# TensorE operands placed at chosen addresses modulo 256 bytes in a gated attention and MLP kernel

## The chip, the cores and the metric

The kernel runs on one core of one Trainium2 chip. The metric is the device time of one execution in microseconds (us). Three runs of the kernel before took 436.31, 436.49 and 436.5 us; their median is 436.49 us. A profile of one further execution is the basis of everything that is read from a trace below.

A core has five engines that work side by side and meet at semaphores: TensorE (PE in the profile; its weight loads have a row of their own, PEld), VectorE (DVE), ScalarE (ACT), GpSimd (POOL) and SyncE (SP), whose queue issues all of this kernel's DMA transfers. SBUF is the on-chip memory of 128 partitions; a tile has an address in bytes within each partition, and it is this address that the change is about. PSUM is the memory that TensorE accumulates into.

A matmul has two operands in SBUF. The **loaded** operand (128 columns here) is put into the array by a weight load before the matmul; the **streamed** operand (448, 450 or 512 columns here) is then passed through it. In the call `nc.tensor.matmul(out, a, w)` the first operand `a` is loaded and the second, `w`, is streamed.

## The reference

Shapes: 2048 tokens of width D = 448, 16 heads of 28, a hidden width F of 1792, everything in fp32.

```python
g = sigmoid((x * gate_w).sum(-1, keepdims=True))
# attention: 8 keys per token at distances 0, 2, 4, ... 14, masked before the start
q, k, v = split(x @ wqkv)                      # 16 heads of 28
logits = einsum("bhsd,bhswd->bhsw", q, k[idx]) * 28 ** -0.5
a = einsum("bhsw,bhswd->bhsd", softmax(mask(logits)), v[idx]) @ wo
# MLP
h = relu(x @ w1 + b1) ** 2
b = h @ w2 + b2
out = g * a + (1 - g) * b
```

## The kernel before

**Arithmetic.** Each fp32 operand is split in two halves of a narrower type (`fp32r`), a rounded one (`...h`) and the remainder (`...l`), and a product is three matmuls: h·h, h·l and l·h. The width of 448 is three blocks of 128 rows and one of 64. The last block is handled with both halves stacked (`x7`, `x8`, `w17`, `wo7`), or, in the qkv projection, by running two matmuls at once on the upper and lower 64 rows of the array.

**Stages.** The 2048 tokens are four chunks of 512.

1. *qkv.* The chunks 0, 1, 2, 3 are projected in this order. Chunk 0 starts with 36 matmuls on the full array (`qkv_first`, line 244); all else, 936 matmuls, is issued by `side_by_side` (line 176) in 468 pairs, one of a pair on array rows 0 to 63 and the other on rows 64 to 127. Loaded are 128 tokens of the chunk (`x.h`, `x.l`, `x7`, `x8`), streamed are `wqh`, `wql`, `w7h`, `w7l`: 450 columns for q (two of them are the gate), 448 for k and v. In chunk 0 both matmuls of a pair mostly stream the same block of the weights for different tokens; in chunks 1 to 3 (`qkv_two`) they stream different blocks. ScalarE copies the results to staging tiles, and SP stores them to DRAM. SP also spills the split x of chunks 0 to 2 to DRAM (`x_d`).
2. *Attention* runs on POOL, DVE and ACT beside the matmuls of the later stages, in pieces that a generator emits by a clock of TensorE's planned time (`advance`). Its outputs are tiles `o`, nine of them.
3. *MLP.* The chunks go in the order 3, 0, 1, 2 (`ORDER`). Chunk 3 is still in SBUF; the others are reloaded from `x_d` by `x_reload` into a ring of five slots (`RING`), four in `xpool` and the fifth in the pool of this stage. For each of 14 blocks f of the hidden width, `mlp_h` (line 620) runs 11 matmuls of 512 columns: loaded is a block of `w1h`, `w1l` or `w17`, streamed is x. ACT and DVE turn the result into `hh` and `hl` (lines 626 to 629), and two blocks later `mlp_o` (line 684) runs 12 matmuls of 448 columns: loaded are `hh` or `hl`, streamed is block f of w2, which lies in `w2ah`, `w2al` for f below 7 and in `w2bh`, `w2bl` from 7 on. One such round of 11 and 12 matmuls is called a step below; there are 56.
4. *Output projection.* Once half of attention is done, each step of MLP also takes one tile of 128 tokens: four transposes (lines 702, 703; streamed is `ident`), and 11 matmuls of 448 columns (line 725; loaded are `oh`, `ol`, `o7`, `o8`, streamed are `woh`, `wol`, `wo7`). Eight tiles go beside chunk 1 of MLP, the other eight after chunk 2, and the last 24 matmuls of MLP come at the end.

The order of the instructions on each engine is written out by the code (`tc.manual_schedule()`); semaphores follow from which tile is read and written. Tiles are placed one after another in the order of the code, pool by pool:

```python
    w1h = const.tile([P, 3, F], F32R, name="w1h")
    b1t = const.tile([P, NF], F32, name="b1t")
    wqh = ap.tile([P, 3, 3, NQ], F32R, name="wqh")
    xt = (xpool if r < 4 else bp).tile([P, 2, CH], F32R, tag=f"x{r}", name=f"x{c}b_{j}")
    w2bh = bp.tile([P, NFA, D], F32R, name="w2bh")
```

The pool `ap` (qkv's weights, x of chunks 0 and 2, the staging tiles) is closed after qkv, and the pool `bp` of MLP takes its place in SBUF; a tile of `bp` waits for the last users of what lay there.

Of the kernel before, what the change touches and what calls it, by code (L numbers as in the profile page):

```python
# [15 lines left out]
P = 128  # L16
# [6 lines left out]
NF = F // P  # L23
CH = 512
NQ = D + 2
SCALE = float(DH) ** -0.5


# [23 lines left out]
def gated_mix_kernel(ctx: ExitStack, tc: tile.TileContext, xT, wqkv, w1, w2, wo, b1, b2, out):  # L52
    nc = tc.nc

    def f32(ap):
        return ap.bitcast(F32)
# [101 lines left out]

    def ncols(b):
        return NQ if b == 0 else D  # L160

    class Acc:

# [25 lines left out]
    def qkv_evacuate(pt, c, tl, b):  # L189
        par, t = c // 2, (c % 2) * 4 + tl  # L190
        first = (b, t // 2) not in stage
        if first:
            stage[b, t // 2] = ap.tile([P, G, 2, C], F32, tag="stage", name=f"st{c}_{tl}_{b}", bufs=ST_BUFS)
        st = stage[b, t // 2]
        nc.scalar.activation(st[:, :, t % 2], pt[:, :D].rearrange("p (g c) -> p g c", g=G), AF.Copy)  # L195
        if not first:
            stage.pop((b, t // 2))
            t0 = t - t % 2
            dst, off = ((q_d, 0), (k_d, HALO), (v_d, HALO))[b]
            dd = dst[par, :, off:off + SP].rearrange("g (p s) c -> p g s c", s=NS)[:, :, t0:t0 + 2]  # L200
            nc.sync.dma_start(dd.rearrange("p g s c -> p g (s c)"), st.rearrange("p g s c -> p g (s c)"))
        if b == 0:
            nc.scalar.activation(zt[:, par, t:t + 1], pt[:, D:D + 1], AF.Copy)

    def full(x, acc, tl, b, ks=range(3)):
        sl, n = slice(tl * P, tl * P + P), ncols(b)
        r = []
        for k in ks:
            r += [(acc, x.h[k][:, sl], wqh[:, k, b, :n]), (acc, x.h[k][:, sl], wql[:, k, b, :n]),
                  (acc, x.l[k][:, sl], wqh[:, k, b, :n])]  # L210
        return r

    def last(x, acc, tl, b):

        sl, n = slice(tl * P, tl * P + P), ncols(b)
# [63 lines left out]
    def halo_ap(d, par, g):  # L279
        base = d[par, g].rearrange("r c -> (r c)")  # L280
        return bass.AP(tensor=base.tensor, offset=base.offset, ap=[[NS * C, P], [1, (NS + HALO) * C]])

    def att_load_qk(par, g):
        q = attp.tile([P, NS, C], F32, tag="q", name=f"q{par}{g}")
        k = attp.tile([P, NS + HALO, C], F32, tag="k", name=f"k{par}{g}")
        nc.sync.dma_start(q, q_d[par, g].rearrange("(p s) c -> p s c", s=NS))
        nc.sync.dma_start(k, halo_ap(k_d, par, g))
        return q, k

    def att_load_v(par, g):  # L290
        v = attp.tile([P, NS + HALO, C], F32, tag="v", name=f"v{par}{g}")
        nc.sync.dma_start(v, halo_ap(v_d, par, g))
        return v

# [54 lines left out]

    def gates(par):  # L350

        e = smp.tile([P, NS], F32, tag="e", name=f"e{par}")
# [152 lines left out]
        raws.append(raw)  # L505
    raw7 = attp.tile([P, D], F32, tag="q", name="wqraw7")
    nc.sync.dma_start(raw7, wqkv[2, :, 3, :D])
    x = x_tiles(0, ap)
    for k in range(3):
        nc.scalar.activation(wqh[:, k, 0], raws[0][:, k, :NQ], AF.Copy)  # L510
        parts = (slice(0, 256), slice(256, CH)) if k == 0 else (slice(0, CH),)
        nc.vector.tensor_copy(x.h[k][:, parts[0]], rx[:, k, parts[0]])
        nc.vector.tensor_sub(wql[:, k, 0], raws[0][:, k, :NQ], f32(wqh[:, k, 0]))  # L513
# [4 lines left out]
    split_full(raws[0][:, 3, :NQ], w7h[:, 0], w7l[:, 0])  # L518
    split_x78(rx[:, 3], x.x7, x.x8)

    def wq_split(b, k):
        if k < 3:
            split_full(raws[b][:, k], wqh[:, k, b, :D], wql[:, k, b, :D])
        else:
            split_full(raw7, w7h[:, 1, :D], w7l[:, 1, :D])

# [77 lines left out]
    def x_reload(i, j):  # L604

        c = ORDER[i]
        r = (4 * i + j) % RING
        xt = (xpool if r < 4 else bp).tile([P, 2, CH], F32R, tag=f"x{r}", name=f"x{c}b_{j}")
        nc.sync.dma_start(f32(xt), x_d[c, j])
        return xt  # L610

    hs = {}

    def mlp_h(x, c, f):
        pt = ps("m", f"h{c}_{f}")
# [5 lines left out]
        return pt  # L621

    def mlp_act(pt, c, f):
        hh = bp.tile([P, CH], F32R, tag="hh", name=f"hh{c}_{f}", bufs=3)
        hl = bp.tile([P, CH], F32R, tag="hl", name=f"hl{c}_{f}", bufs=3)
        nc.scalar.activation(pt, pt, AF.Relu, bias=b1t[:, f:f + 1])  # L626
        nc.scalar.activation(hh, pt, AF.Square)  # L627
        nc.scalar.activation(pt, pt, AF.Square)  # L628
# [140 lines left out]

    pend = []  # L770
    early = RING - 4
    nxt = []
# [74 lines left out]
```

## Time and profile before

| | |
|---|---|
| median of three runs | 436.49 us |
| the profiled execution, its own time | 436.64 us |
| its span, from the first instruction to the last | 434.9 us |
| PE busy | 429.1 us (99% of the span), 2516 matmuls |
| PEld busy | 385.9 us (89%) |
| POOL, DVE, ACT busy | 274.8, 257.9, 179.3 us |
| granted TensorE clock, mean over the span | 0.998 |

The page of the profile gives busy times of the engines, the span in 40 slices, the DMA queues, the chain of work that ended last, the costliest groups of instructions by line, and the DMA issues. Matmuls overlap in the record (each is shown from its first column to its last result), so the mean duration of one is longer than the distance to the next. What a matmul costs where PE never waits is that distance. The view that shows it is the chain of waits in order of time: while the chain runs on PE, a piece such as "PE b L684 x12" gives when the piece began and how long these 12 matmuls held the chain.

### The profile page before, as it was taken

The numbers are of one execution on the slowest core, as the hardware profiler recorded it, in microseconds if no ns is written. First come the engines' busy times: TensorE is split into PE (matmuls) and PEld (weight loads), VectorE is DVE, ScalarE is ACT, GpSimd is POOL, SyncE is SP. The second block draws the span as 40 slices with busy tenths as digits, with TensorE's granted clock in tenths as the row PEclk, the third lists the DMA queues.
The fourth block names the chain that finished last, engine by engine and source line by source line (L and its number), as shares of the span: only waits on it lengthen the run. The fifth ranks groups of instructions, "written<-read, shape, count | busy, mean of one in ns | idle before, by whom it ended". The sixth has DMA issues, their size and how long they took to land.

```text
span 434.9 us, 6554 instructions
## 1 busy us (share of the span) xinstructions
PE 429.1 (99%) x2516; PEld 385.9 (89%) x2516; DVE 257.9 (59%) x384; ACT 179.3 (41%) x372; POOL 274.8 (63%) x167
## 2 busy tenths in 40 slices
PE   8999999999999999999999999999999999999996
PEld 7999999999888888888888888888888888888895
DVE  4421322375589977976646776644676856755453
ACT  3542454444554444533433454333523433334530
POOL 1000001940999999999998897945499998785000
PEclk9999999999999999999999999999999999999999
DMA  7989899938723307703203651401427400210013
GB/s 224 365 299 346 223 391 287 356 80 298 260 89 119 142 2 259 254 29 121 78 2 121 223 199 36 151 21 44 142 86 260 172 1 0 76 68 0 2 63 128
DMA packets 33199, 65.44 MB, mean 150 GB/s; under 512 B 2704, under 2 KB 26256, under 8 KB 32784
## 3 DMA queue, kind: packets, MB, share of 16 engines
q1 hardware_dynamic: 33168, 65.02, 43.0%
q8 instruction: 20, 0.33, 0.3%
q14 instruction: 11, 0.09, 0.1%
HBM read 41.23 MB, written 23.77 MB: 149 GB/s over the span
## 4 chain that ended last, share of the span: by engine, by line
PE 97%; DMA 1%; DVE 1%; SPq 0%; issue 0%; ACT 0%
PE h L620 33%; PE b L684 31%; PE qkv L176 22%; PE a L725 8%; PE oT L702 1%; PE qkv L244 1%; DMA xraw<-xT 1%; PE oT L703 0%; SPq L499 0%; SPq L494 0%; DVE bt L660 0%; DVE wql L513 0%; DVE x L514 0%; DVE ol L102 0%; ACT o L101 0%
## 5 line engine op out<-in xcount | busy, mean ns | idle before, releaser
L308 POOL TENSOR_TENSOR qk<-q,k 128x896 f32<-128x896 f32 x64 | 138.6, 2193 | 103.4 <-DMA k<-k_d 72.5
L315 POOL TENSOR_TENSOR av<-lg,v 128x896 f32<-128x896 f32 x64 | 122.3, 2006 | 13.2 <-DVE o L321 7.1
L626 ACT ACTIVATE h<-h,b1t 128x512 f32<-128x512 f32 x56 | 37.0, 662 | 157.6 <-PE h L620 157.6
L176 PE MATMUL qkv<-wqh,x 64*128 64x448 f32 (+1 forms) x528 | 86.8, 363 | 0.0
L629 DVE TENSOR_TENSOR hl<-h,hh 128x512 fp32r<-128x512 f32 x56 | 38.6, 688 | 62.1 <-ACT h L628 61.9
L309 DVE TENSOR_REDUCE lg<-qk 128x32 f32<-128x896 f32 x64 | 66.9, 1076 | 3.9 <-POOL qk L308 3.9
L321 DVE TENSOR_REDUCE o<-av 128x112 f32<-128x896 f32 x64 | 66.6, 1072 | 0.0
L176 PEld LDWEIGHTS qkv<-wqh,x 64*128 64x128 f32 x528 | 59.6, 185 | 0.6
L176 PE MATMUL qkv<-wql,x 64*128 64x448 f32 (+1 forms) x264 | 56.5, 363 | 0.0
L195 ACT ACTIVATE st<-qkv 128x448 f32<-128x448 f32 x48 | 24.7, 544 | 48.4 <-PE qkv L176 39.9
L684 PE MATMUL b<-w2bl,hh 128*128 128x448 f32 x112 | 40.9, 365 | 0.0
L684 PE MATMUL b<-w2bh,hl 128*128 128x448 f32 x112 | 40.9, 365 | 0.0
L684 PE MATMUL b<-w2bh,hh 128*128 128x448 f32 x112 | 40.9, 365 | 0.0
L684 PE MATMUL b<-w2ah,hh 128*128 128x448 f32 x112 | 40.7, 364 | 0.0
L684 PE MATMUL b<-w2ah,hl 128*128 128x448 f32 x112 | 40.6, 362 | 0.0
L684 PE MATMUL b<-w2al,hh 128*128 128x448 f32 x112 | 40.5, 362 | 0.0
L627 ACT ACTIVATE hh<-h 128x512 fp32r<-128x512 f32 x56 | 33.6, 599 | 3.6 <-DMA v_d<-st 1.9
L628 ACT ACTIVATE h<-h 128x512 f32<-128x512 f32 x56 | 33.2, 593 | 0.0
L176 PEld LDWEIGHTS qkv<-wql,x 64*128 64x128 f32 x264 | 30.8, 185 | 0.3
L620 PE MATMUL h<-x1b,w1h 128*128 128x512 f32 x84 | 28.6, 395 | 0.0
L620 PE MATMUL h<-x2b,w1h 128*128 128x512 f32 x84 | 28.5, 393 | 0.0
L620 PE MATMUL h<-x0b,w1h 128*128 128x512 f32 x84 | 28.4, 391 | 0.0
(108 smaller groups left out, 761.0 us busy)
## 6 DMA issues: line engine op xcount, KB each, us to landing
k<-k_d SPq DMA_DIRECT2D x8, 840.0 KB, 5.1
v<-v_d SPq DMA_DIRECT2D x8, 840.0 KB, 4.6
x_d<-x SPq DMA_DIRECT2D x12, 512.0 KB, 5.5
q_d<-st SPq DMA_DIRECT2D x8, 448.0 KB, 8.0
k_d<-st SPq DMA_DIRECT2D x8, 448.0 KB, 5.1
v_d<-st SPq DMA_DIRECT2D x8, 448.0 KB, 6.7
w1raw<-w SPq DMA_DIRECT2D x4, 896.0 KB, 9.9
q<-q_d SPq DMA_DIRECT2D x8, 448.0 KB, 3.4
```

The source lines that it names most:

```text
L176: nc.tensor.matmul(acc.pt[:, :acc.n], a[rows], w[rows], start=acc.todo == 21, stop=acc.todo == 1)
L308: nc.gpsimd.tensor_mul(pr, q[:, s:s + 1].to_broadcast([P, W, C]), k[:, s:s + W])
L309: pending.append(lambda: nc.vector.tensor_reduce(lg[:, s], pr.rearrange("p w (h d) -> p w h d", h=HG), axis=AX.X, op=ALU.add))
L315: nc.gpsimd.tensor_mul(pr.rearrange("p (h d) w -> p w h d", h=HG), lg[:, s][:, :, :, None].to_broadcast([P, W, HG, DH]), v[:, s:s + W].rea ...
L321: pending.append(lambda: nc.vector.tensor_reduce(o[:, g * C:(g + 1) * C], pr, axis=AX.X, op=ALU.add))
L620: nc.tensor.matmul(pt, w, a, start=i == 0, stop=i == len(pr) - 1)
L626: nc.scalar.activation(pt, pt, AF.Relu, bias=b1t[:, f:f + 1])
L627: nc.scalar.activation(hh, pt, AF.Square)
L628: nc.scalar.activation(pt, pt, AF.Square)
L629: at(HL_DELAY, lambda: nc.vector.tensor_sub(hl, pt, f32(hh)))
L684: nc.tensor.matmul(bps[tl][:, :D], a[:, sl], w, start=f == 0 and i == 0, stop=f == NF - 1 and i == 2)
L725: nc.tensor.matmul(pa[:, :D], a, w, start=i == 0, stop=i == len(pr) - 1)
```

## The change

All of it is about where tiles lie. The instructions of TensorE, VectorE, ScalarE and GpSimd are the same ones in the same order with the same shapes. On SP's queue one transfer changes its place: the first reload of x (the first of chunk 0) is issued before the load of w2's row 4 instead of after it, and takes over its wait for the end of qkv on TensorE.

- `wqh` and `wql` get one row of 512 + 2·448 columns for each k block instead of three blocks of 450, and `w7h`, `w7l` one of 512 + 448; the new `block(b)` gives the columns of a block. Every block then starts at the same address modulo 256 bytes.
- `b1t`, the gates (`zt`, `gt`, `g1t`, now parts of one tile `zg`), the tiles of k and v, and `e` are padded to multiples of 256 bytes, and three empty tiles (`pad_x`, `pad_a`, `pad_b`) shift what lies behind them.
- Pools are split, so that x and the staging tiles of qkv (`xap`), MLP's weights with the fifth slot of the ring (`bw`), and `hh`, `hl` (`hp`) can be shifted apart.
- The nine tiles `o` move from a pool of their own, kept through the whole kernel, to MLP's pool `bp`.

Where the operands then start, modulo 256 bytes, as the two programs place them:

| operand | its part | before | after |
|---|---|---|---|
| `wqh`, `wql` (line 176, 244) | streamed | 64, 72, 80 ... 128 and 160, 168 ... 224, by block | 128 |
| `w7h`, `w7l` (line 176) | streamed | 0, 8, 32, 40 | 128 |
| x of chunks 0 and 2 in qkv | loaded | 64 | 64 |
| x of chunks 1 and 3 in qkv | loaded | 128 | 128 |
| `w1h`, `w1l`, `w17` (line 620) | loaded | 128 | 128 |
| x of chunk 3, four slots of the ring (line 620) | streamed | 128 | 128 |
| fifth slot of the ring: block 0 of chunk 0, block 1 of chunk 1, block 2 of chunk 2 (3 of the 11 matmuls of a step each) | streamed | 64 | 128 |
| `hh`, `hl` (line 684) | loaded | 64 | 64 |
| `w2ah`, `w2al` (f below 7) | streamed | 128 | 128 |
| `w2bh`, `w2bl` (f from 7 on) | streamed | 64 | 128 |
| `oh`, `ol`, `o7`, `o8` (line 725); `o`, `od` (lines 702, 703) | loaded | 64 | 64 |
| `woh`, `wol`, `wo7` (line 725) | streamed | 64 | 128 |
| `ident` (lines 702, 703) | streamed | 192 | 128 |

```diff
+NP = 512
...
-    b1t = const.tile([P, NF], F32, name="b1t")
+    b1t = const.tile([P, 64], F32, name="b1t")[:, :NF]
...
-    zt = const.tile([P, 2, NS], F32, name="zt")
-    gt = const.tile([P, 2, NS], F32, name="gt")
-    g1t = const.tile([P, 2, NS], F32, name="g1t")
-
+    zg = const.tile([P, 8, NS], F32, name="zg")
+    zt, gt, g1t = zg[:, 0:2], zg[:, 2:4], zg[:, 4:6]
+
+    const.tile([P, 64], F32, name="pad_x")
...
-    opool = ctx.enter_context(tc.tile_pool(name="opool", bufs=1))
...
+    xap = actx.enter_context(tc.tile_pool(name="phase_a_x", bufs=1, reuse_waits="tile"))
...
-    wqh = ap.tile([P, 3, 3, NQ], F32R, name="wqh")
-    wql = ap.tile([P, 3, 3, NQ], F32R, name="wql")
-
-    w7h = ap.tile([P, 2, NQ], F32R, name="w7h")
-    w7l = ap.tile([P, 2, NQ], F32R, name="w7l")
+    wqh = ap.tile([P, 3, NP + 2 * D], F32R, name="wqh")
+    wql = ap.tile([P, 3, NP + 2 * D], F32R, name="wql")
+
+    w7h = ap.tile([P, NP + D], F32R, name="w7h")
+    w7l = ap.tile([P, NP + D], F32R, name="w7l")
+    ap.tile([P, 48], F32, name="pad_a")
...
+    def block(b):
+
+        o = (0, NP, NP + D)[b]
+        return slice(o, o + ncols(b))
...
-            stage[b, t // 2] = ap.tile([P, G, 2, C], F32, tag="stage", name=f"st{c}_{tl}_{b}", bufs=ST_BUFS)
+            stage[b, t // 2] = xap.tile([P, G, 2, C], F32, tag="stage", name=f"st{c}_{tl}_{b}", bufs=ST_BUFS)
...
-            r += [(acc, x.h[k][:, sl], wqh[:, k, b, :n]), (acc, x.h[k][:, sl], wql[:, k, b, :n]),
-                  (acc, x.l[k][:, sl], wqh[:, k, b, :n])]
+            r += [(acc, x.h[k][:, sl], wqh[:, k, n]), (acc, x.h[k][:, sl], wql[:, k, n]),
+                  (acc, x.l[k][:, sl], wqh[:, k, n])]
...
-        h, l = w7h[:, b // 2, :n], w7l[:, b // 2, :n]
+        sl = slice(tl * P, tl * P + P)
+        n = block(1) if b == 2 else slice(0, ncols(b))
+        h, l = w7h[:, n], w7l[:, n]
...
+    def kv_tile(tag, name):
+        n = (NS + HALO) * C
+        return attp.tile([P, n + 48], F32, tag=tag, name=name)[:, :n].rearrange("p (s c) -> p s c", c=C)
...
-    x = x_tiles(0, ap)
+    x = x_tiles(0, xap)
...
-        xs[c] = x_tiles(c, xpool if c % 2 else ap)
+        xs[c] = x_tiles(c, xpool if c % 2 else xap)
...
+    bw = ctx.enter_context(tc.tile_pool(name="weights_b", bufs=1, reuse_waits="tile"))
+    hp = ctx.enter_context(tc.tile_pool(name="hidden", bufs=3, reuse_waits="tile"))
     bp = ctx.enter_context(tc.tile_pool(name="phase_b", bufs=1, reuse_waits="tile"))
-    w2bh = bp.tile([P, NFA, D], F32R, name="w2bh")
-    w2bl = bp.tile([P, NFA, D], F32R, name="w2bl")
-    woh = bp.tile([P, 3, D], F32R, name="woh")
-    wol = bp.tile([P, 3, D], F32R, name="wol")
-    wo7 = bp.tile([P, D], F32R, name="wo7")
+    opool = bp
+    w2bh = bw.tile([P, NFA, D], F32R, name="w2bh")
+    w2bl = bw.tile([P, NFA, D], F32R, name="w2bl")
+    woh = bw.tile([P, 3, D], F32R, name="woh")
+    wol = bw.tile([P, 3, D], F32R, name="wol")
+    wo7 = bw.tile([P, D], F32R, name="wo7")
...
-        xt = (xpool if r < 4 else bp).tile([P, 2, CH], F32R, tag=f"x{r}", name=f"x{c}b_{j}")
+        xt = (xpool if r < 4 else bw).tile([P, 2, CH], F32R, tag=f"x{r}", name=f"x{c}b_{j}")
...
+    nxt = [x_reload(1, j) for j in range(RING - 4)]
+    bw.tile([P, 48], F32, name="pad_b")
...
-        hh = bp.tile([P, CH], F32R, tag="hh", name=f"hh{c}_{f}", bufs=3)
-        hl = bp.tile([P, CH], F32R, tag="hl", name=f"hl{c}_{f}", bufs=3)
+        hh = hp.tile([P, CH], F32R, tag="hh", name=f"hh{c}_{f}")
+        hl = hp.tile([P, CH], F32R, tag="hl", name=f"hl{c}_{f}")
...
-        if i < 3:
+        if 0 < i < 3:
             nxt = [x_reload(i + 1, j) for j in range(early)]
```

More of the change, by code (lines that the diff above doesn't have):

```diff
@@ L205, in full @@
     def full(x, acc, tl, b, ks=range(3)):
-        sl, n = slice(tl * P, tl * P + P), ncols(b)
+        sl, n = slice(tl * P, tl * P + P), block(b)
         r = []
         for k in ks:
-            r += [(acc, x.h[k][:, sl], wqh[:, k, b, :n]), (acc, x.h[k][:, sl], wql[:, k, b, :n]),
-                  (acc, x.l[k][:, sl], wqh[:, k, b, :n])]
+            r += [(acc, x.h[k][:, sl], wqh[:, k, n]), (acc, x.h[k][:, sl], wql[:, k, n]),
+                  (acc, x.l[k][:, sl], wqh[:, k, n])]
         return r
     def last(x, acc, tl, b):
-        sl, n = slice(tl * P, tl * P + P), ncols(b)
-        h, l = w7h[:, b // 2, :n], w7l[:, b // 2, :n]
+        sl = slice(tl * P, tl * P + P)
+        n = block(1) if b == 2 else slice(0, ncols(b))
+        h, l = w7h[:, n], w7l[:, n]
         return [(acc, x.x7[:, sl], h), (acc, x.x7[:, sl], l), (acc, x.x8[:, sl], h)]
@@ L281, in halo_ap @@
         return bass.AP(tensor=base.tensor, offset=base.offset, ap=[[NS * C, P], [1, (NS + HALO) * C]])
+    def kv_tile(tag, name):
+        n = (NS + HALO) * C
+        return attp.tile([P, n + 48], F32, tag=tag, name=name)[:, :n].rearrange("p (s c) -> p s c", c=C)
     def att_load_qk(par, g):
         q = attp.tile([P, NS, C], F32, tag="q", name=f"q{par}{g}")
-        k = attp.tile([P, NS + HALO, C], F32, tag="k", name=f"k{par}{g}")
+        k = kv_tile("k", f"k{par}{g}")
         nc.sync.dma_start(q, q_d[par, g].rearrange("(p s) c -> p s c", s=NS))
@@ L290, in att_load_v @@
     def att_load_v(par, g):
-        v = attp.tile([P, NS + HALO, C], F32, tag="v", name=f"v{par}{g}")
+        v = kv_tile("v", f"v{par}{g}")
         nc.sync.dma_start(v, halo_ap(v_d, par, g))
@@ L350, in gates @@
     def gates(par):
-        e = smp.tile([P, NS], F32, tag="e", name=f"e{par}")
+        e = smp.tile([P, 32], F32, tag="e", name=f"e{par}")[:, :NS]
         nc.scalar.activation(e, zt[:, par], AF.Exp, scale=-1.0)
@@ L507, in gated_mix_kernel @@
     nc.sync.dma_start(raw7, wqkv[2, :, 3, :D])
-    x = x_tiles(0, ap)
+    x = x_tiles(0, xap)
     for k in range(3):
-        nc.scalar.activation(wqh[:, k, 0], raws[0][:, k, :NQ], AF.Copy)
+        nc.scalar.activation(wqh[:, k, :NQ], raws[0][:, k, :NQ], AF.Copy)
         parts = (slice(0, 256), slice(256, CH)) if k == 0 else (slice(0, CH),)
         nc.vector.tensor_copy(x.h[k][:, parts[0]], rx[:, k, parts[0]])
-        nc.vector.tensor_sub(wql[:, k, 0], raws[0][:, k, :NQ], f32(wqh[:, k, 0]))
+        nc.vector.tensor_sub(wql[:, k, :NQ], raws[0][:, k, :NQ], f32(wqh[:, k, :NQ]))
         nc.vector.tensor_sub(x.l[k][:, parts[0]], rx[:, k, parts[0]], f32(x.h[k][:, parts[0]]))
@@ L517, in gated_mix_kernel @@
             nc.vector.tensor_sub(x.l[k][:, cols], rx[:, k, cols], f32(x.h[k][:, cols]))
-    split_full(raws[0][:, 3, :NQ], w7h[:, 0], w7l[:, 0])
+    split_full(raws[0][:, 3, :NQ], w7h[:, :NQ], w7l[:, :NQ])
     split_x78(rx[:, 3], x.x7, x.x8)
@@ L522, in wq_split @@
         if k < 3:
-            split_full(raws[b][:, k], wqh[:, k, b, :D], wql[:, k, b, :D])
+            split_full(raws[b][:, k], wqh[:, k, block(b)], wql[:, k, block(b)])
         else:
-            split_full(raw7, w7h[:, 1, :D], w7l[:, 1, :D])
+            split_full(raw7, w7h[:, NP:], w7l[:, NP:])
     def when(t, fn, *args):
```

1 line of the change is left out of this document (removed).

## The prediction, made before the changed kernel was run

> **What bounds the kernel now.** I read the page first (busy times, the chain's shares), then the chain of waits in order of time, then the waits of PE.
>
> ```profile
> span 434.9 us, 6554 instructions
> PE 429.1 (99%) x2516; PEld 385.9 (89%) x2516; DVE 257.9 (59%) x384; ACT 179.3 (41%) x372; POOL 274.8 (63%) x167
> PE 97%; DMA 1%; DVE 1%; SPq 0%; issue 0%; ACT 0%
> PE warm L487 <- DVE zero L485: 1.2, 1, 1.2
> ```
>
> PE is busy for 99% of the span, 97% of the chain is PE, and the only wait of PE that the view of waits lists is 1.2 us before the warm-up. So the time is the number of matmuls times their distance, and only that distance can change where the instructions stay the same. It is read from the chain, whose columns are start, us held, what:
>
> ```profile
> 13.81 95.86 PE qkv L176 x928
> 109.67 7.70 PE h L620 x33
> ...
> 124.67 2.49 PE h L620 x11
> 127.16 2.40 PE b L684 x12
> ...
> 149.13 2.49 PE h L620 x11
> 151.62 2.43 PE b L684 x12
> 154.06 2.52 PE h L620 x11
> ...
> 171.44 7.29 PE b L684 x36
> 178.73 7.60 PE h L620 x33
> ...
> 193.67 2.53 PE h L620 x11
> ...
> 248.00 7.64 PE h L620 x33
> ...
> 258.05 2.56 PE h L620 x11
> 260.61 0.33 PE oT L702 x3
> 260.94 0.11 PE oT L703
> ...
> 263.46 2.57 PE h L620 x11
> ...
> 266.47 2.23 PE a L725 x11
> 268.70 2.41 PE b L684 x12
> ...
> 339.06 7.61 PE h L620 x33
> ...
> 349.07 2.54 PE h L620 x11
> ...
> 403.64 0.33 PE oT L702 x3
> ...
> 425.77 4.88 PE b L684 x24
> ```
>
> The reader is to see that the same 11 matmuls cost 2.49, 2.52, 2.53, 2.54, 2.56 or 2.57 us, and the same 12 cost 2.40 or 2.43. Against the table of addresses: 2.40 is w2's first half (streamed at 128), 2.43 its second half (at 64). 2.49 is chunk 3 beside that first half, when every streamed operand of MLP starts at 128; 2.52 is the same chunk with the second half between; 2.53 and more are the chunks with three of 11 matmuls on the fifth slot (at 64). No DMA, wait or clock stands between these rows. So the streamed address bears on the distance, and a matmul streamed at 64 also lengthens those after it: in chunk 3 all 11 are streamed at 128 in both 2.49 and 2.52.
>
> **The change, part by part.** All sums are made against the profiled execution: 436.64 us, of which 434.9 is the span. The median of the runs shown is 0.15 us lower; the difference found here is taken off the median.
>
> *MLP.* After the change every step has the addresses that the five steps from 124.67 to 149.13 have now: 24.46 us, 4.892 per step, of which 2.40 are b and 2.492 are h (226.5 ns per matmul of 512 columns, 200.0 per one of 448). By chunks, from the starts of the chain's pieces:
> - Chunk 3 takes 178.73 - 109.67 = 69.06. I leave the first three h (7.70, with the entry from qkv) as they are; 11 more at 2.492 and 14 b at 2.40 give 68.71: **-0.35**.
> - Chunk 0 takes 248.00 - 178.73 = 69.27; 14 steps of 4.892 are 68.49: **-0.78**.
> - Chunk 1 takes 339.06 - 248.00 = 91.06, with eight tiles of transposes (0.44 each) and of projection (a, 2.23 each). a is 11 matmuls of 448 columns, loaded at 64, streamed at 64 now and at 128 after, as b; 11 at 200.0 ns are 2.20. So 68.49 + 3.52 + 17.60 = 89.61: **-1.45**. The transposes' `ident` moves from 192 to 128, which no row here prices; I take nothing. They would have to move by the whole 8 ns by which the h rows differ per matmul, over 64 of them, to matter by 0.5 us either way.
> - Chunk 2 runs from 339.06 to 403.64, 64.58, with 12 of its 14 b; 68.49 - 4.80 = 63.69: **-0.89**.
> - The end: eight more a, 8 x 0.03, and the last 24 b, 4.88 to 4.80: **-0.32**.
>
> Together -3.79. Something is given back where the transposes break the even stream: the b right after one shows 2.41 for 2.40. Taken as 0.01 to 0.02 for each of 16 tiles, it is +0.2, so **-3.6**.
>
> *qkv.* 95.86 us for 468 pairs are 204.8 ns per pair. Here no row shows the new state, since the blocks now start at many residues and hardly ever two in a row at 128. Upper gain: each half of the array goes as b does at 128, 200.0 ns for 448 columns (336 per half) and 200.9 for 450 (132 per half, scaled by the columns): 93.72, so -2.1. The other end: the pairs lose what separates the best from the worst h row, (2.57 - 2.49) / 11 = 7 ns, 468 times, +3.4. The nearest rows are b's, with the same 448 columns: 200.0 streamed at 128, 202.5 at 64. qkv's 204.8 lies above both, as a stage of uneven addresses would, so I take two thirds of the way to the lower end: **-1.4**. A loss would need two streams at one residue to disturb each other. Two windows of the qkv stage speak to that (columns: window, us, PE busy and matmuls, PEld, clock, DMA share, GB/s):
>
> ```profile
> 14.00:32.20 18.20, 18.20 (x180) 17.78 (x180) 1.00 0.89 327
> 32.20:57.95 25.75, 25.75 (x254) 25.48 (x253) 1.00 0.90 296
> ```
>
> Chunk 0, where most pairs stream one and the same block in both halves, takes 18.20 / 180 = 101.1 ns per matmul; chunk 1, where the two differ, 25.75 / 254 = 101.4. Equal residues cost nothing visible.
>
> *The first full-array matmuls of qkv and the warm-up* (before 13.81) stand in the chain between DMA waits; nothing is taken.
>
> *SP's queue.* The reload of x moves ahead of w2's row 4 and takes its wait for TensorE, after which the same queue goes on.
>
> ```profile
> 110.78 0.46 SPq L201 DMA_DIRECT2D v_d<-st  x1
> 111.33 0.86 SPq L601 DMA_DIRECT2D w2raw<-w  x1
> 112.28 1.15 SPq L609 DMA_DIRECT2D x0b<-x_d  x1
> w2raw<-w SPq DMA_DIRECT2D x10, 224.0 KB, 5.2
> 117.66 0.56 ACT L101 ACTIVATE w2ah<-w2raw 128x448 fp32r<-128x448 f32 x1
> 122.30 0.66 ACT L626 ACTIVATE h<-h,b1t 128x512 f32<-128x512 f32 x1 [1.61 <-PE h L620]
> ```
>
> The wait itself costs nothing: qkv ends at 109.67, before the queue gets there at 111.33. Row 4 is then issued 1.15 us later and lands near 117.7 or, behind 512 KB, some us later, while ACT wants it at 117.66 and is in order: behind it stand the activations of h. That delay is covered twice: ACT idles 1.61 us before the next h, and what it makes of h is used by PE some 9 us later (the b at 127.16). Row 4 itself is first streamed some 10 us after that. It would show only if the landing slipped by over 6 us; nothing is taken. The tiles `o`, `hh` and `hl` lie in other places, where the last users were qkv and w2's loads, done before their first writes; no wait of POOL, DVE or ACT becomes a later one.
>
> *Attention's cover.* A shorter PE could run into attention's end.
>
> ```profile
> 382.19 14.89 POOL L315 TENSOR_TENSOR av<-lg,v 128x896 f32<-128x896 f32 x8 [1.66 <-DMA v<-v_d]
> 398.67 2.07 DVE L321 TENSOR_REDUCE o<-av 128x112 f32<-128x896 f32 x2
> ```
>
> The last two outputs are reduced by 400.74; the tiles before them much earlier. PE takes the first transpose at 403.64, and the last tile of the eight some 17 us later. A shift of 5 us leaves the last one 12 us.
>
> **Sum:** -3.6 - 1.4 = -5.0: 436.64 becomes 431.6, and on the median 436.49 - 5.0 = **431.5 us**.
>
> **A rule against it.** The Trainium skill ("TensorE: Matmul & The Clock Gate", section "Back-to-back issue gap") gives the distance of warm matmuls as N / 2.4 + 2.5 ns, from the number of columns alone, and its step-by-step section says that a weight load takes nothing from the running matmul's reads. By that estimate 512 columns are 215.8 ns and 448 are 189.2, wherever the operands lie, and this change moves nothing: 436.5. The trace disagrees: 226.5 and 200.0 at best, and 2.49 against 2.57 us for the same eleven.
>
> **The rivals.**
> 1. *The addresses do little: about 436.5.* The steps would differ by what lies in other tiles (which slot, which weights), not by the residue. For it: slot and residue change together in this kernel, so the fifth slot is both. Against it: b shows the same sign with other tiles, and 2.52 appears in chunk 3 with unchanged x.
> 2. *The even stream holds only where nothing interrupts it: 433.5.* The eight h after transposes stay at 2.57 instead of 2.49, 8 x 0.08 = 0.64, and qkv with its two streams gains nothing: 5.0 - 0.64 - 1.4 = 3.0 us gained. For it: 2.57 stands beside the transposes. Against it: 2.56 (at 258.05) stands ahead of the first transpose (260.61).
> 3. *Slower, by qkv: about 439.7.* Streams that both start at 128 meet in the same part of memory at the same moment and hold each other up. The point from which it decides is 3.6 / 468 = 7.7 ns per pair, so a pair over 212.5. At twice the spread of the h rows, 14.5 ns per pair, it costs 6.8: 436.49 - 3.6 + 6.8. For it: all residues are made equal, which today they are not. Against it: the two windows above.
>
> **How the numbers follow.** A measurement of this kernel can tell about 0.2%, 0.9 us, from no change. Forecast 0.80, its own range 430.6 (qkv at -2.1, nothing given back) to 432.9 (qkv at 0); rival 2 0.11; rival 1 0.04; rival 3 0.05. Faster is the forecast and rival 2, 0.91; the same 0.04; slower 0.05. The range, 430.4 to 433.9, holds the forecast and rival 2.
>
> **What would show it.** Right: in the chain all h x11 after the first chunk's entry at 2.49, all b x12 at 2.40, a x11 at 2.20, and qkv near 94.5 us. Wrong: w2's second half still at 2.43 (then it was not the residue); h at 2.57 only beside transposes (rival 2); qkv at or above 95.9 (its term is void, above 99.5 rival 3); a wait of PE on ACT near 118 to 128 us (SP's swap); a wait on attention's outputs after 398 us.

## The result and the profile after

The changed kernel takes 432.62 us (median; 432.42 to 433.07), the kernel before 436.44 us beside it: a ratio of 0.9914 with a 95% interval of 0.9897 to 0.9932. That is 3.8 us less, where 5.0 us had been forecast. The profiled execution took 432.75 us, its span is 431.0 us.

The page of the changed kernel (the span; busy times of the engines; shares of the chain), and one row of its view of waits (who waited for whom: us, times, longest):

```profile
span 431.0 us, 6553 instructions
PE 424.9 (99%) x2516; PEld 384.4 (89%) x2516; DVE 265.5 (62%) x384; ACT 179.4 (42%) x372; POOL 272.1 (63%) x167
PE 81%; POOL 9%; DVE 6%; issue 2%; DMA 1%; ACT 0%; SPq 0%; DVEq 0%; POOLq 0%
PE b L703 <- DVE hl L648: 0.2, 1, 0.2
```

Before, 97% of the chain was PE. Now 15% of it runs over POOL and DVE, and PE waits once for `hl`. So something else has come to the front for a part of the span. The chain of waits of the changed kernel (start, us held, what):

```profile
13.27 95.39 PE qkv L185 x931
108.67 5.20 PE h L639 x22
...
118.91 5.98 DVE w2al L104
...
184.78 0.61 DVE hl L648
185.43 2.27 PE b L703 x10
187.71 2.49 PE h L639 x11
190.20 2.40 PE b L703 x12
...
246.33 7.48 PE h L639 x33
...
276.66 2.54 PE h L639 x11
...
314.53 2.49 PE h L639 x11
317.02 2.20 PE a L744 x11
...
336.23 7.48 PE h L639 x33
```

In MLP the steps are those that were forecast: h at 2.49, b at 2.40 with either half of w2, a at 2.20. Some h after transposes read 2.50 to 2.55. Two things are not as forecast: qkv holds 95.39 us, not 94.5, and between 113.9 and 185.4 us the chain leaves PE.

The sum over the two profiled executions, from the starts of the chain's pieces: up to the first pair of qkv 13.81 to 13.27, -0.54; qkv 95.86 to 95.39, -0.47; from there to the last transposes (109.67 to 403.64 before, 108.67 to 399.94 after) 293.97 to 291.27, -2.70; the rest of the span 31.26 to 31.06, -0.20. Together -3.91, the difference of the spans to 0.01.

qkv by chunks, each window from the start of a chunk's first pair to that of the next (columns: window, us, PE busy and matmuls, clock, DMA share, GB/s). First the kernel before:

```profile
13.81:32.28 18.47, 18.47 (x182) 1.00 0.89 328
32.28:58.03 25.75, 25.75 (x256) 1.00 0.91 298
58.03:83.78 25.75, 25.75 (x256) 1.00 1.00 340
83.78:109.67 25.89, 25.89 (x254) 1.00 0.63 209
```

and the changed kernel:

```profile
13.27:31.40 18.13, 18.13 (x182) 1.00 0.93 336
31.40:57.13 25.73, 25.73 (x256) 1.00 0.91 295
57.13:82.50 25.37, 25.37 (x255) 1.00 0.99 336
82.50:108.66 26.16, 26.16 (x255) 1.00 0.66 219
```

Chunks 0 and 2 gain 0.34 and 0.38 us. Chunk 1 gains nothing and chunk 3 loses 0.27. All four stream the weights at 128 now. What differs is the loaded operand: x lies at 64 in chunks 0 and 2 (pool `phase_a_x`), at 128 in chunks 1 and 3 (`xpool`). The clock is full in all of them.

### The profile page after: what moved, and what is told of

It reads as the page before. It is cut to its first block, busy times and chain, and to the rows that moved or that the text cites. A ratio compares the mean times of both kernels' runs of the same rounds, so it can differ in the third digit from the quotient of the medians.

```text
span 431.0 us, 6553 instructions
## 1 busy us (share of the span) xinstructions
PE 424.9 (99%) x2516; PEld 384.4 (89%) x2516; DVE 265.5 (62%) x384; ACT 179.4 (42%) x372; POOL 272.1 (63%) x167
## 4 chain that ended last, share of the span: by engine, by line
PE 81%; POOL 9%; DVE 6%; issue 2%; DMA 1%; ACT 0%; SPq 0%; DVEq 0%; POOLq 0%
PE h L639 24%; PE b L703 23%; PE qkv L185 22%; PE a L744 8%; POOL av L329 4%; POOL qk L322 4%; PE qkv L254 2%; DVE w2al L104 1%; DVE wol L104 1%; PE oT L721 1%; DMA xraw<-xT 1%; DVE o L335 1%; DVE hl L648 1%; DVE bt L679 1%; POOL lg L360 0%
## 5 line engine op out<-in xcount | busy, mean ns | idle before, releaser
L329 POOL TENSOR_TENSOR av<-lg,v 128x896 f32<-128x896 f32 x64 | 120.2, 1977 | 13.0 <-DVE o L335 7.1
L185 PE MATMUL qkv<-wqh,x 64*128 64x448 f32 (+1 forms) x528 | 90.4, 362 | 0.0
L185 PEld LDWEIGHTS qkv<-wqh,x 64*128 64x128 f32 x528 | 73.4, 184 | 1.0
L185 PE MATMUL qkv<-wql,x 64*128 64x448 f32 (+1 forms) x264 | 74.1, 361 | 0.0
L185 PEld LDWEIGHTS qkv<-wql,x 64*128 64x128 f32 x264 | 44.4, 184 | 0.5
L639 PE MATMUL h<-x,w1h 128*128 128x512 f32 x84 | 28.2, 390 | 0.0
```

Source lines behind the costliest of these rows:

```text
L185: nc.tensor.matmul(acc.pt[:, :acc.n], a[rows], w[rows], start=acc.todo == 21, stop=acc.todo == 1)
L329: nc.gpsimd.tensor_mul(pr.rearrange("p (h d) w -> p w h d", h=HG), lg[:, s][:, :, :, None].to_broadcast([P, W, HG, DH]), v[:, s:s + W].rea ...
L639: nc.tensor.matmul(pt, w, a, start=i == 0, stop=i == len(pr) - 1)
```

## Experiments

The theory after the result: what counts is not where the streamed operand starts but by how much its address differs, modulo 256, from that of the loaded one. The rivals: the streamed residue alone (the prediction's reading), the place (which tile and slot), and for what is missing, a wait that isn't an address at all.

### The two residues by themselves

```diff
+RES = (("z", 0), ("q", 16), ("h", 32), ("t", 48))     # floats: 0, 64, 128, 192 bytes
+for what, n, kind in ((whole, 448, "f"), (whole, 512, "g"), (pairs, 448, "p")):
+    for ln, l in RES:                                  # loaded
+        for sn, s in RES:                              # streamed
+            what(n, s, l, f"{kind}_s{sn}_l{ln}")       # 40 matmuls
```

> This kernel leaves out the whole computation: it runs only chains of 40 matmuls on fixed operands, one chain for each pair of residues modulo 256 bytes (streamed operand and loaded operand at 0, 64, 128 or 192), with 448 columns on the full array, with 512 columns on the full array, and with 448 columns in pairs on the two halves of the array. Its output is zeros. My theory (both residues count): streamed at 128 and loaded at 64 gives 200.0 ns per matmul of 448 columns; streamed at 128 and loaded at 128 gives 226.7 for 512 and 206.5 for the pairs; streamed at 64 and loaded at 64 gives 202.8 for 448; streamed at 64 and loaded at 128 gives 233.3 for 512. Rival (only the streamed operand counts, as in the prediction): within one streamed residue the four loaded residues are equal, 200.0 and 226.7 at 128. Rival (it was never the residue): all 16 chains of a shape are equal within 1 ns.

The chain of waits of that kernel, full array (start, us held by 40 matmuls, name; in a name, `s` is the streamed and `l` the loaded operand, and `z`, `q`, `h`, `t` stand for 0, 64, 128 and 192):

```profile
61.18 8.00 PE f_sh_lq L54 x40
...
93.58 8.26 PE f_sh_lh L54 x40
101.84 8.00 PE f_st_lh L54 x40
...
206.68 9.28 PE g_st_lq L54 x40
...
234.58 9.09 PE g_sh_lh L54 x40
243.67 9.17 PE g_st_lh L54 x40
```

With 448 columns, streamed 128 over loaded 64 and 192 over 128 take 8.00 us for 40: the difference is 64 both times, whatever the two are. 128 over 128 takes 8.26. With 512 columns it is the other way: a difference of 0 has the shortest chain (9.09), one of 64 takes 9.17, one of 128 9.28. From the starts of the matmuls, for differences of 0, 64, 128 and 192: 206.7 (or 202.7 in some chains), 200.0, 204.0 and 202.1 ns for 448 columns, 226.7, 228.9, 232.0 and 233.4 ns for 512. The pairs on half arrays give the same.

This explains qkv: at a difference of 64 the changed kernel's 448-column matmuls run at 200.0 ns (chunks 0 and 2), at 0 in chunks 1 and 3 at up to 206.5, slower than before the change (their means there are 204.5 and 206.4, before 203.9 and 203.8).

### The addresses between

```diff
+for n, kind in ((448, "f"), (512, "g")):
+    for d in range(0, 64, 4):                  # floats: 0 to 240 bytes
+        whole(n, d, 0, f"{kind}_d{d * 4}")
+for d in range(0, 64, 16):
+    whole(450, d, 0, f"e_d{d * 4}")
+    pairs(450, d, 0, f"q_d{d * 4}")
```

> Leaves out the whole computation: chains of 40 matmuls, each with its own loaded operand, streamed from an address 0 to 240 bytes (in steps of 16) past the loaded one's residue modulo 256; 448 and 512 columns on the full array, 450 columns on the full array and in pairs on half arrays at steps of 64. Theory (the distance of two matmuls is a step function of the difference of the two residues): the steps of 64 repeat the earlier grid (448 columns 206.7, 200.0, 203.7 and 202.1 ns, 512 columns 226.7, 228.9, 232.0 and 233.4 ns), and the addresses between lie between or on them. Rival A (a finer interleaving of the addresses decides): some step of 16 or 32 is well below 200.0 or 226.7 ns, and a better placement than the changed kernel's exists. Of 450 columns the theory says nothing; if they follow 448 columns, the difference of 64 is again the shortest, at about 200.9 ns.

Measured, ns from start to start in the second half of each chain of 40:

| difference | 0 | 16 | 32 | 48 | 64 | 80 | 96 | 112 | 128 | 144 | 160 | 176 | 192 | 208 | 224 | 240 |
|---|---|---|---|---|---|---|---|---|---|---|---|---|---|---|---|---|
| 448 columns | 202.6 | 200.0 | 204.4 | 202.9 | 199.9 | 203.3 | 205.4 | 206.7 | 204.0 | 206.7 | 200.0 | 204.4 | 202.0 | 204.0 | 204.4 | 202.6 |
| 512 columns | 226.6 | 231.7 | 233.3 | 233.3 | 229.0 | 230.9 | 233.4 | 231.4 | 232.4 | 233.3 | 234.4 | 231.2 | 233.3 | 234.7 | 233.4 | 226.6 |

Nothing lies below 200.0 or 226.6, so no finer step beats what the changed kernel has in MLP. 450 columns (q's block with the gate) don't follow 448: in pairs the last matmuls run at 203.4, 206.7, 204.0 and 206.7 ns for 0, 64, 128 and 192. So the difference that suits the 448-column matmuls of qkv costs the others, some three tenths, a few ns, and no pair chain here held the forecast's floor of 200.9 for 450 columns. That isn't settled by one chain of each: on the full array the chain of 450 at 64 ran at 206.8 in its first half and at 200.0 in its second.

### Undo the new address of w2's second half, wo and the fifth slot

```diff
     opool = bp
+    bw.tile([P, 48], F32, name="pad_b")
     w2bh = bw.tile([P, NFA, D], F32R, name="w2bh")
...
     nxt = [x_reload(1, j) for j in range(RING - 4)]
-    bw.tile([P, 48], F32, name="pad_b")
```

> The changed kernel with one pad moved from the end of MLP's weight pool to its beginning, so that w2's second half, wo and the fifth slot of x start at 64 modulo 256 again, 192 bytes from where they were, and all else stays. Residue theory: the b of the second half return to 2.43 us, a to 2.23, h of chunks 0 to 2 to 2.53 to 2.57, qkv keeps its 95.4; some 3.3 us of the gain go, about 435.7 us. Rival (tiles or pools moved, not the residue): all rows stay at 2.40, 2.21 and 2.49, 432.6 us.

436.34 us (436.02 to 436.74), ratio 0.999 [0.9978, 1.0002]: with the tiles still in their new pools, the time is that of before. Only the pairs of qkv, which this leaves alone, keep their 95.39 us. (It is 0.6 us more than expected; the first pair starts at 13.93 here, 0.66 later than in the changed kernel.) The chain:

```profile
263.09 2.57 PE h L639 x11
...
266.10 2.23 PE a L744 x11
...
306.57 2.43 PE b L703 x12
```

The old 2.57, 2.23 and 2.43 are back. The place is not the cause.

### Move the loaded operand alone

```diff
-    bw.tile([P, 48], F32, name="pad_b")
```

This moves `hh`, `hl`, `o`, `oh` and the like from 64 to 128, and no streamed operand.

> The changed kernel without that pad: hh, hl, the attention outputs and the projection's loaded operands start at 128 instead of 64, everything streamed stays at 128. Theory (the loaded residue counts, and 128 is the bad one for 448 columns): b goes from 2.40 to about 12 x 206.5 ns = 2.48 and a from 2.21 to 2.27, 56 x 0.08 + 16 x 0.06 = 5.4 us more, about 438.0 us. Rival (what qkv shows is peculiar to pairs on the halves of the array): b stays at 2.40, 432.6 us.

436.16 us (435.7 to 440.14), ratio 0.9998 [0.9976, 1.002]. The chain:

```profile
268.05 2.43 PE b L702 x12
270.48 2.50 PE h L638 x11
...
275.68 2.48 PE b L702 x12
```

A kernel whose operands are all streamed at 128 is as slow as the one before: b takes 2.43 or 2.48 instead of 2.40. So the streamed residue alone doesn't decide, and with the grid the difference does. The loss is smaller than expected because nearly all b take the lower of the grid's two distances at a difference of 0: 2.43 is 202.7 ns each, and only three of the b beside the transposes hold 2.48, 206.7 ns each, which the expectation had for all.

### Move w1 alone

```diff
+    const.tile([P, 48], F32, name="pad_w")
     w1h = const.tile([P, 3, F], F32R, name="w1h")
...
+    const.tile([P, 16], F32, name="pad_v")
     NFA = NF // 2
```

> The changed kernel with w1 alone put at 64 instead of 128, x streamed at 128 as it is. Theory (the difference of streamed and loaded residue decides): the difference becomes 64, the grid's 228.9 instead of 226.7 ns, so 616 distances of h cost 2.2 ns more each, steps of h read 2.51 to 2.52 instead of 2.49, and the time is 432.6 + 1.4 = 434.0 us. Rival A (what counts is where the streamed operand lies, as the prediction's sum had it): h stays at 2.49 and the time at 432.6 us. Rival B (a loaded operand at 64 is good for itself, as it is for 448 columns): h gets shorter, 431.5 us.

434.32 us (434.28 to 434.45), ratio 0.9947 [0.9934, 0.996]. All but one of the h that stand alone in the chain read 2.52 or 2.53 (the one 2.54), and their 616 distances sum to 141.34 us against 139.92, +1.42 where the grid's 2.2 ns each made 1.36. w1 at 128 is right for h though 64 is right for b: the two have different numbers of columns.

### Load x at 64 in chunk 1

```diff
+    def x_slot(j, name, off=0):
+        t = xpool.tile([P, 2 * CH + 64], F32R, tag=f"x{j}", name=name)
+        return t[:, off:off + 2 * CH].rearrange("p (a c) -> p a c", a=2)
...
+        return X([x_slot(j, f"x{c}_{j}", 48 if c == 1 else 0) for j in range(4)])
```

> The changed kernel with chunk 1's x placed 192 bytes further in its four slots (which grow by 256 bytes), so that qkv loads it at 64 instead of 128; the reloads for MLP use the slots at 128 as before. Theory (the loaded residue makes the odd chunks of qkv slow): chunk 1 goes from 25.7 us to what chunk 2 has, 25.4; about 432.3 us. Rival (chunks 1 and 3 are slow because of what runs beside them, or because x lies in another pool): chunk 1 stays at 25.7, 432.6 us.

433.7 us (432.39 to 436.14; its runs scatter), ratio 0.9936 [0.9905, 0.9967]. The pairs, between windows cut as above, go from 95.39 to 95.19 us: chunk 1 from 25.73 to 25.44, as expected, while chunk 2 behind it gives 0.10 back (25.37 to 25.47), at the same addresses. The time can't show 0.2 us in this scatter; the chunk's window does.

### x and w1 at 64 everywhere, with and without wo's rows moved

```diff
+    const.tile([P, 48], F32, name="pad_w")
     w1h = const.tile([P, 3, F], F32R, name="w1h")
...
+    const.tile([P, 16], F32, name="pad_v")
     NFA = NF // 2
...
-    const.tile([P, 64], F32, name="pad_x")
+    const.tile([P, 48], F32, name="pad_x")
...
+    padp.tile([P, 16], F32, name="pad_y")
...
+    bw.tile([P, 48], F32, name="pad_b")
     hs = {}
     nxt = [x_reload(1, j) for j in range(RING - 4)]
-    bw.tile([P, 48], F32, name="pad_b")
...
-        at(50000.0 + k * 4500.0, lambda k=k: wo_row(k))     # second kernel only
+        at(85000.0 + k * 4500.0, lambda k=k: wo_row(k))
```

> The changed kernel with x at 64 in all four chunks and w1 at 64 with it; everything else stays. So q, k and v load at 64 and stream at 128 everywhere (difference 64 also in chunks 1 and 3), while h streams at 64 and loads at 64 (difference 0 as before). Theory: chunks 1 and 3, now 25.7 us to a half each, fall to chunk 2's 25.4, 0.3 us each; h keeps 2.49; 432.6 - 0.6 = 432.0 us, or 432.2 if chunk 2 gives back what it did in the run with chunk 1 alone. Rival A (the distances of q, k and v are set by the evacuations beside them, not by addresses): 95.4 us of pairs and 432.6 us stay. Rival B (128 is a good address for a streamed operand for itself): h at 64 goes to 2.55 or more, 616 distances by 5 ns, 435.7 us or more.

> The kernel with x and w1 at 64 everywhere, and besides the three rows of wo loaded and split some 35 us later, so that VectorE isn't in their subtraction when it should make hl for the first step of b. Theory (the 0.45 us that PE stands at 185 us is the price of VectorE being held up beside GpSimd): the wait of b for hl goes, and the time is that of x and w1 at 64 without it, 432.1 - 0.45 = 431.6 us. Rival A (another VectorE job takes that place): a wait of the same size shows elsewhere in chunk 0, and the time is the same as with wo early. Rival B (wo comes too late, or its DMA holds up x's reload): a wait of a or of h for wo or x, 432.5 us or more.

434.5 us (433.19 to 434.71), ratio 0.9941 [0.9927, 0.9956], and with wo's rows later 433.56 us (433.31 to 435.29), ratio 0.9935 [0.9921, 0.9949]. The pairs do fall to 94.85 us, the expected 0.55 less. But h gets longer, which the theory didn't have and rival B had larger and for another reason. With wo's rows later, no b waits for `hl` any more, as that theory said; the time stays above its 431.6 us because the distances of h sum to 140.75 us there against the changed kernel's 139.92. From the chain of the first of the two:

```profile
208.25 2.52 PE h L643 x11
```

h is at a difference of 0 here as in the changed kernel, and takes 2.52 instead of 2.49. From start to start the eleven of such a step run at 231, 236, 228, 232, 231, 227, 227, 226, 227, 227 and 226 ns: slow at first, then at the old distance. In the changed kernel, away from the transposes, all eleven are at 226 or 227. The new thing is that b streams at 128 and h at 64, so the streamed residue changes at each step.

### The change of the streamed residue by itself

```diff
+def steps(sb, lb, sh, lh, name):                       # in floats
+    for i in range(6):
+        whole(448, sb, lb, f"b_{name}", 12)
+        whole(512, sh, lh, f"h_{name}", 11)
+for name, r in (("after", (32, 16, 32, 32)), ("all", (32, 16, 16, 16)), ("zero", (32, 16, 0, 0)),
+                ("last", (32, 16, 48, 48)), ("back", (16, 16, 32, 32)), ("low", (16, 0, 32, 32)),
+                ("same", (16, 0, 16, 16)), ("wone", (32, 16, 32, 16))):
+    steps(*r, name)
```

> Leaves out the whole computation: steps of 12 matmuls of 448 columns (as b) and 11 of 512 (as h) in turn, six of each, for eight sets of residues (streamed/loaded of b, then of h): after 128/64, 128/128; all 128/64, 64/64; zero 128/64, 0/0; last 128/64, 192/192; back 64/64, 128/128; low 64/0, 128/128; same 64/0, 64/64; wone 128/64, 128/64. Theory (two things count: the difference inside a step, and whether the streamed residue stays the same from step to step, since after a change of it the first four or five matmuls of h run at 229 to 236 ns until they are at 226.7 again): after and same hold 2.40 and 2.49 us; all, zero, last and low have b at 2.40 and h at 2.51 to 2.53; back has b at 2.43 and h at 2.52 to 2.53; wone has h at 2.52 by its difference of 64, with no slow start. Rival (128 is a good residue of a streamed operand for itself): same is no better than all, and low and back have h at 2.49.

The chain of that kernel, one b and one h of each of five sets, and the first h of two of them:

```profile
32.02 2.40 PE b_after L53 x12
34.42 2.49 PE h_after L53 x11
...
44.20 2.49 PE h_all L53 x11
...
61.48 2.41 PE b_all L53 x12
63.88 2.52 PE h_all L53 x11
...
150.52 2.43 PE b_back L53 x12
152.96 2.52 PE h_back L53 x11
...
180.25 2.41 PE b_low L53 x12
182.67 2.54 PE h_low L53 x11
...
192.57 2.54 PE h_same L53 x11
...
200.00 2.40 PE b_same L53 x12
202.40 2.49 PE h_same L53 x11
```

"same" streams everything at 64 and is as fast as "after", which streams everything at 128: 128 is not good for itself. "low" has the same h as "after", streamed at 128 and loaded at 128, and takes 2.54; the b before it streams at 64. "back" differs from "after" in b's streamed residue alone and is what the kernel before has in w2's second half, 2.43 and 2.52. "zero" and "last" came out at 2.54, a little above the expected 2.53, and "wone" at 2.52 to 2.53 by its difference of 64.

So two things count: the difference inside a step, which sets the steady distance, and, where steps repeat, a streamed residue that stays the same from step to step. The changed kernel's MLP keeps both. The second is no strict rule, as the first step of a set shows: in "all" the first h goes from 128 to 64 and still holds 2.49 (at 44.20), and in "same" the first h takes 2.54 (at 192.57) though the b right before it streams at 64 as well. In the changed kernel itself, five h of chunk 1, where the transposes stand, begin slow with everything streamed at 128: the eleven at 276.66 run at 235, 234, 235, 225, 230, 236, 229, 232, 231, 227 and 230 ns. What puts an h into the slow start is thus not known; a change of the streamed residue that comes back at every step did it in every step but that first one.

### qkv by both rules

The last three kernels ran beside each other: the changed kernel as it is, the same with wq's split weights at 192 and x at 128 in all chunks (a difference of 64 everywhere, and MLP untouched), and that with wo's rows later.

```diff
+    ap.tile([P, 16], F32, name="pad_q")
     wqh = ap.tile([P, 3, NP + 2 * D], F32R, name="wqh")
...
-        at(50000.0 + k * 4500.0, lambda k=k: wo_row(k))     # third kernel only
+        at(85000.0 + k * 4500.0, lambda k=k: wo_row(k))
```

> The changed kernel as it is, beside the next two on one chip: 432.6 us, pairs of q, k and v 95.4 us, and PE waiting some 0.4 us for hl at 185 us.

> The changed kernel with wq's split weights (wqh, wql, w7h, w7l) at 192 instead of 128 and x at 128 in chunks 0 and 2 as in 1 and 3, so that q, k and v have a difference of 64 in all four chunks, while everything that MLP streams stays at 128. Theory (difference, and one streamed residue through MLP): chunks 1 and 3 go from 25.7 to about 25.4 us, the pairs from 95.4 to 94.85 as with all at 64, h stays at 2.49; 432.6 - 0.55 = 432.1 us. Rival (the gain of the pairs is given back by what follows, as with all at 64): 432.6 us or more.

> As the kernel with wq at 192, and wo's rows loaded and split 35 us later. Theory: PE's wait for hl at 185 us goes, 0.45 us: 432.1 - 0.45 = 431.65 us. Rival (the wait moves to another place in chunk 0): as with wo early, 432.1 us.

| kernel | us (runs) | ratio to before, 95% interval | pairs of qkv, us |
|---|---|---|---|
| changed | 433.25 (432.97 to 433.49) | 0.9919 [0.9906, 0.9932] | 95.39 |
| wq at 192 | 433.16 (432.44 to 434.02) | 0.9916 [0.9902, 0.9930] | 94.85 |
| wq at 192, wo later | 431.99 (431.75 to 432.14) | 0.9890 [0.9876, 0.9904] | 94.85 |

The pairs do what the rules say, 0.55 us less, and the time does not follow until wo is moved: 433.16 us is the rival's outcome. Why, the view of waits and the chain of the kernel with wq at 192 show:

```profile
PE b L704 <- DVE hl L649: 0.7, 1, 0.7
185.19 0.61 DVE hl L649
```

The changed kernel makes `hl` from 184.78 on, this one from 185.19: DVE is not earlier because PE is, so PE stands longer (0.7 us by that view, 0.2 in the changed kernel). The matmul distances of all b show the loss without that view's rounding: above their steady distance by 0.54 us in the changed kernel, 1.02 with wq at 192, 0.09 with wo later. The wait is thus about 0.45 us in the first and 0.9 in the second. With wo later the chain has no piece of another engine between the first pair and the first transposes:

```profile
108.53 7.68 PE h L640 x33
...
177.23 7.48 PE h L640 x33
...
245.74 7.48 PE h L640 x33
```

Where DVE falls behind is seen in its timeline at 118 us. First the changed kernel, then the one with wo later (start, us, engine, line, operation):

```profile
118.08 6.33 POOL L322 TENSOR_TENSOR qk<-q,k 128x896 f32<-128x896 f32 x3
118.83 6.06 DVE L104 TENSOR_TENSOR w2al<-w2raw,w2ah 128x448 fp32r<-128x448 f32 x1
```

```profile
118.42 7.08 POOL L323 TENSOR_TENSOR qk<-q,k 128x896 f32<-128x896 f32 x3
118.92 2.12 DVE L104 TENSOR_TENSOR w2al<-w2raw,w2ah 128x448 fp32r<-128x448 f32 x1
```

One subtraction of 448 columns takes 6.06 us beside three POOL instructions and ends 0.48 us after the last of them (124.89 against 124.41); its like takes 2.12 in the other kernel and took 1.38 before the change. In all eleven traces of the whole kernel it ends 0.48 to 0.49 us after one of these three multiplications, after the first where it is short and after the third where it is long. In all kernels run, a subtraction of 6.04 to 6.31 us at this place (the changed kernel twice, w1 at 64, x at 64 in chunk 1, x and w1 at 64, wq at 192) goes with the chain over DVE to 185 us, and one of at most 2.12 us (w2 and wo undone, loaded operands at 128, both kernels with wo later) with none. That the long subtraction is the cause is read from the chain, which passes through it; no run changed it alone, and in the kernels with w2 and wo undone and with loaded operands at 128 PE is slower as well, which leaves `hl` more time. These two have the swapped reload on SP's queue too, so the swap by itself doesn't make the subtraction long. Why wo's rows, which come 50 us later, decide which of the two happens is open: in both kernels POOL begins 0.5 to 0.75 us ahead of DVE, and at a lead of 0.74 to 0.76 us both cases occur (w2 and wo undone 1.86 us, the changed kernel 6.06). The changed kernel with wo later and nothing else wasn't run.

## Why the prediction was right, and where it was not

**The bound.** That the matmuls' distance is what changes the time held: it carries the whole gain but the start's. That nothing else could come to bound it did not: the argument that DVE is off the path looked at the end of attention (398 us) and not at the middle, where `hl` had been ready some 0.9 us ahead of PE (185.5 against 186.4 us in the trace before). PE was 1.4 us earlier there (0.54 at the start, 0.47 in qkv, 0.36 in chunk 3), and DVE with its long subtraction was not. This is the forecast's missing term: +0.45 us.

**MLP.** The terms were right to a few hundredths. Chunks 3 and 0 were forecast at 68.71 and 68.49; without the wait (the kernel with wo later) they hold 177.23 - 108.53 = 68.70 and 245.74 - 177.23 = 68.51. In the changed kernel chunk 1 holds 89.90 (336.23 - 246.33) against 89.61, which is the 0.2 given back and 0.1 more; the h after transposes pay it, not the b. Chunk 2 is 63.71 against 63.69. The end brought 0.20 of 0.32.

**qkv.** The step that failed: "The nearest rows are b's ... 200.0 streamed at 128, 202.5 at 64", and from them -1.4. Measured -0.47: the term was mis-sized by 0.93 us, the largest miss of the sum. The rows were right and read by the wrong variable: b at 2.43 was streamed at 64 over operands loaded at 64, a difference of 0. By the difference, chunks 1 and 3 had no gain to expect, and with the right difference the whole of qkv gains 1.0 (95.86 to 94.85), since 450 columns in pairs want another one. That b and h rows differed in two residues each was in the table of addresses and not used.

**The start.** Taken as 0; the profiled executions differ by -0.54. The profiled executions of the changed kernel and of its variants put the first pair at 13.27 to 14.10 us, on both sides of the 13.81 before, so this is scatter and no part of the change that can be shown. It is luck that it hid a third of what the other terms fell short: against the forecast, qkv is off by +0.93 us, the wait by +0.45, MLP without it by +0.12, the end by +0.12 and the start by -0.54, together 1.08, and -5.0 becomes -3.9. The changed kernel's second set of runs shows 3.5 us of gain (433.25 against 436.72).

**"A matmul streamed at 64 also lengthens those after it."** Right as a reading. In steps that repeat, the first five to ten matmuls after a change of the streamed residue are slow, whether it goes to 64 or from it (231, 236, 228, 232, 231 and then 226 or 227 with x and w1 at 64). Why, and why some h begin slow without a change, stays open.

**The swap in SP's queue** cost nothing that the waits show: PE waits on no ACT at 118 to 128 us.

**The rule of the Trainium skill** ("TensorE: Matmul & The Clock Gate", section "Back-to-back issue gap"), N / 2.4 + 2.5 ns from the columns alone, which that section gives for the gap of an isolated matmul, does not hold here: 448 columns took 200.0 to 206.7 ns and 512 took 226.6 to 234.7, at the same number of columns and by their addresses. Moving the loaded operand alone took b from 2.40 to 2.43 or 2.48 us.

**The rivals.** "The addresses do little" fell with the kernel that undoes them (436.34). "Only where nothing interrupts it": the h after transposes are at 2.50 to 2.55, not at 2.57, and pay about 0.2 of its 0.64 us; that qkv would gain next to nothing was nearer than the forecast, for another reason than two streams. "Slower by qkv": pairs at 95.39 / 468 = 203.8 ns, where over 212.5 was needed.

## What to carry to other kernels

Where TensorE is busy all the time, take the address of both operands of each matmul modulo 256, and compare the same instruction between steps in the chain: place the pair by its difference for that number of columns (here 64 bytes for 448, 0 for 512), and keep one streamed residue through steps that alternate. Then read the matmuls from start to start, since the same addresses did not always give the same distance here. Before a saving on the bounding engine is booked in full, look up at each point how far ahead the other engines are, not only at the end; here a margin of 0.9 us took back half a microsecond, and after the next step nearly all that the step had saved.

## What the runs showed of the hardware

- The distance of matmuls depends on (streamed - loaded) modulo 256, between 200.0 and 206.7 ns for 448 columns (on full and on half arrays alike) and between 226.6 and 234.7 for 512. The shortest, 200.0 and 226.7, are 26.7 ns apart for 64 columns, 0.417 ns each; by that, an estimate from these two, both are the time of 32 columns more than were streamed. A chain of 450 columns reached 200.0 too, so it isn't exact.
- The same addresses can hold two steady distances: 202.7 or 206.7 ns at a difference of 0 with 448 columns, and a chain of 450 columns at 64 that went over to 200.0 ns halfway. What decides isn't shown: 448 columns at 0 over 0, right after the same warm-up, ran at 206.7 in one kernel and at 202.6 in another.
- In steps that repeat, a change of the streamed residue costs h 25 to 50 ns (2.52 to 2.54 against 2.49 us) and b up to 15 (2.415 against 2.40).
- A DVE subtraction of two SBUF operands took 1.38, 2.12 or 6.06 us at the same place. Each time it ended 0.48 us after one of the three POOL multiplications beside it, the first or the third; which of them, no run explains. Over seven such subtractions the mean went from 790 to 1607 ns by a change that left the operations of both engines as they were:

```profile
L102 DVE TENSOR_TENSOR w2al<-w2raw,w2ah 128x448 fp32r<-128x448 f32 x7 | 5.5, 790 | 3.3 <-ACT w2ah L101 3.3
```

(the groups by line of the kernel before), and of the changed kernel:

```profile
L104 DVE TENSOR_TENSOR w2al<-w2raw,w2ah 128x448 fp32r<-128x448 f32 x7 | 11.2, 1607 | 3.3 <-ACT w2ah L103 3.3
```
